# Last token group of a mixture of MLPs: second product by two nested Strassen levels

## The chip, the cores and the metric

The kernel runs on one core of a Trainium2 chip. The metric is the device time of one execution in microseconds, from the first instruction to the last. The kernel before takes 1227.81 us (median of three runs, 1226.56 to 1229.82). All arithmetic is in fp32.

The engines are named as in the profile: PE is the matrix engine, PEld its weight loads, DVE the vector engine, ACT the scalar engine, POOL the GpSimd engine, SP the engine that here only issues transfers. Each works through its own queue in order and waits on semaphores. PSUM is the memory that PE writes (8 banks of 128 x 512 fp32), SBUF the working memory, DRAM the device's main memory.

## The reference

Attention makes x, and four expert MLPs are applied to every token, mixed by normalised probabilities:

```python
def _moe_ref(x, domain_probs, w1, w2):          # x: 3072 x 512, w1: 4 x 512 x 1024, w2: 4 x 1024 x 512
    p = domain_probs / (domain_probs.sum(-1, keepdims=True) + 1e-09)
    out = np.zeros((N, D), dtype=np.float32)
    for e in range(E):
        h = np.maximum(x @ w1[e], 0.0)
        out += p[:, e:e + 1] * (h @ w2[e])
    return out
```

x comes from a decayed linear attention (4 batches, 8 heads, 768 positions, 64 per head), computed in blocks. The change doesn't touch it.

## The kernel before

**Tiling.** The 3072 tokens are three groups (`g`) of 1024. A group and an expert (`e`) make a unit, of which there are twelve, in the order (0,0), (0,1), ... (2,3). A unit has two matrix products: the first gives the hidden values h, transposed (1024 features x 1024 tokens), the second gives the outputs (1024 tokens x 512).

**Strassen.** A product of two matrices cut in 2 x 2 blocks can be done with seven block products M1 to M7 instead of eight, if sums of blocks are made first and the results are added up afterwards. `A_OF` and `B_OF` say which block or sum is an operand of which product (S1 to S4 are sums of left blocks, T1 to T4 of right blocks). The *first product* (`first_product`, L537) uses this twice, one inside the other: 7 outer products M, each of 7 inner ones (`inner`, L548), and each inner product is two matmuls of 128 x 128 by 128 x 256. Its operands with all their sums are prepared ahead by Pool (`prepare_w1`, L170; `prepare_x`, L236), written to DRAM (`inner`, L138, whose stores go out on ACT's queue) and read back by `feed` (L480). PE writes the PSUM banks pg; the values are added into SBUF tiles m by DVE (L93, called from `inner`), or copied by ACT where a sum begins (L563), and ReLU is applied by ACT (L567, L509).

The *second product* (`second_product`, L592) uses one level: 7 products, each of four parts (L594) of four matmuls, with h or its sums hS as the left operand (from `operands`, L458, on DVE) and w2 or its sums as the right (`prepare_w2`, L202; read by `feed2`, L577, 512 KB per product). A part is 128 tokens x 256 outputs. DVE scales it by the gate of the token, which stands on the partitions here, and adds it into the accumulators acc (L620, L623). After the last expert the accumulators are stored from Pool's queue (L626).

**The order of the work** is written out by hand. The loop over units at L734 pairs the second product of one unit with the first product of the next. It goes through seven steps `i`, one M of each; a step has eight slots, in which pieces of the two products alternate on PE (`order`, L755). After each slot one piece of background work runs on DVE (`rest`, L343: sums for S blocks, and sums that the outer Strassen level needs), every second slot `pump` (L127) issues pending stores and one chore of the operand preparation, and one step of the attention of a later group is put in where there is one. The attention of group 2 lies beside the units (0,3) to (1,1). The unit (2,3) has no first product beside it: it stands alone at the end.

**Buffers.** `stage` has 7 buffers of 128 x 1024 for preparing operands, `w2` has 6 for right operands, `stream` has 2 of each kind for the operands of the first product, `o` has 8 of 128 x 512 for acc, `pool` has 47 of 128 x 512 for everything else. Second products use the PSUM banks q01, q02, q11, q12, first products g1 and g3, attention s0 and s1.

`tt` (L92, its instruction on L93) is the helper for all sums of two tensors, so in the profile one line, L93, stands for many places. The tiles tell them apart.

Of the kernel before, what the change touches and what calls it, by code (L numbers as in the profile page):

```python
# [10 lines left out]
ALU = mybir.AluOpType  # L11
AX = mybir.AxisListType
FP32 = mybir.dt.float32
# [7 lines left out]
def kernel(  # L21
# [95 lines left out]
    x_ops = dram.tile([NG, 7, P, 7, 256], FP32, name="x_ops")  # L117
    w2_sums = dram.tile([E, 4, P, 2, W], FP32, name="w2_sums")

    W1_AT = {n: i for i, n in enumerate(("M1", "M7", "M6", "M5", "M3", "M2", "M4"))}  # L120
# [45 lines left out]
    def inner_x(eng, g, m, blk):  # L166
        at = {"B11": (0, 0), "B12": (0, 1), "B21": (1, 0), "B22": (1, 1)}
        inner(eng, ("x", g, m), x_ops[g, MS.index(m)], blk, T_OPS, at)

    def prepare_w1(e):  # L170
        st = {}

        def block(name, i, j):
            t = stage.tile([P, 2, W], FP32, name="w1b", tag="st")
            src = moe_w1[e, j * 256:(j + 1) * 256, i * W:(i + 1) * W]
            nc.sync.dma_start(out=t[:], in_=src.rearrange("(c p) f -> p c f", p=P))
            st[name] = t

        def total(name, a, b, op):
            t = stage.tile([P, 2, W], FP32, name="w1o", tag="st")  # L180
            tt(nc.gpsimd, t[:], st[a][:], st[b][:], op)
            st[name] = t

        def ready(m):
            inner_w1(e, m, st[A_OF[m]])

        return [
            lambda: (block("A11", 0, 0), block("A21", 1, 0), block("A22", 1, 1)),
            lambda: ready("M1"),
            lambda: total("S1", "A21", "A22", ALU.add), lambda: ready("M5"),  # L190
            lambda: total("S3", "A11", "A21", ALU.subtract), lambda: ready("M7"),
            lambda: (total("S2", "S1", "A11", ALU.subtract), block("A12", 0, 1)), lambda: ready("M6"),
            lambda: ready("M2"),
            lambda: total("S4", "A12", "S2", ALU.subtract), lambda: ready("M3"),
            lambda: ready("M4"),
        ]

# [4 lines left out]
    def prepare_w2(e):  # L202
# [8 lines left out]
        def total(name, n, a, b, op):  # L211
# [14 lines left out]
            lambda: total("T4", 3, "B21", "T2", ALU.subtract),  # L226
        ]

    SUM_AT = {"T1": 0, "T2": 1, "T3": 2, "T4": 3}
# [94 lines left out]
    gate = consts.tile([P, NTOK // P, E], FP32, name="gate")  # L324

    def gates():
        total = consts.tile([P, NTOK // P], FP32, name="total")
# [12 lines left out]

    background = []

    def rest(n=1):  # L343
        for _ in range(min(n, len(background))):
            background.pop(0)()

# [128 lines left out]


    SEQ = ("M1", "M5", "M6", "M2", "M7", "M3", "M4")
    fed = {}

    def feed(g, e, m):  # L480
        if (g, e, m) in fed:
            return
        while ("x", g, m) not in made and background:
            rest()
        until(("x", g, m))
# [6 lines left out]

    INNER = ("M1", "M7", "M6", "M4", "M5", "M2", "M3")

# [7 lines left out]
    def finished(g, e, m, blocks, new):  # L502

        def later(to, a, b, order, relu=False):
            def step(at):
                o = to[at] if at in to else small("m" + at)
                tt(nc.vector, o[:], a[at][:], b[at][:], ALU.add)
                if relu:
                    nc.scalar.activation(out=o[:], in_=o[:], func=AF.Relu)  # L509
                to[at] = o  # L510
                blocks["left"] -= 1
# [3 lines left out]

        def keep(c, i, j):
            hid[g, e, i, j] = {"A11": c["11"], "A12": c["21"], "A22": c["22"], "A21": c["12"]}
            operands((g, e, i, j))
# [13 lines left out]
    def settle(m, blocks):  # L532

        while m in ("M7", "M4") and blocks["left"]:
            rest()

    def first_product(g, e, m, blocks, tags):  # L537
# [10 lines left out]
        def inner(i):  # L548
# [17 lines left out]
            if m in OUT and (at == "12" or not begins):  # L566
                nc.scalar.activation(out=new[at][:], in_=new[at][:], func=AF.Relu)  # L567

        return [lambda i=i: inner(i) for i in INNER] + [lambda: finished(g, e, m, blocks, new)]
# [22 lines left out]
    def second_product(g, e, m, banks):  # L592

        def part(sj, s):  # L594
# [7 lines left out]
            for uu in range(2):  # L602
                h = hid[g, e, uu, sj]
                while A_OF[m] not in h:
                    rest()
                for c in range(2):
# [17 lines left out]
            if e == E - 1 and m in ("M2", "M4", "M5", "M3"):  # L624
                queue = nc.sync if (g, m) == (NG - 1, "M3") else nc.gpsimd
                queue.dma_start(out=out[n * P:(n + 1) * P, j * DH:(j + 1) * DH], in_=o)  # L626

# [6 lines left out]

        return [lambda sj=sj, s=s: part(sj, s) for s in range(2) for sj in (1, 0)] + [done]


# [93 lines left out]
    fill = [(*u, m) for u in units[2:] for m in SEQ]  # L731
    fill2 = [(*u, m) for u in units for m in SEQ2]
    steps = attention(1)
    for at, (g, e) in enumerate(units):  # L734
        if (g, e) == (0, 1) or (g, e) == (0, 2):
            chores.extend(prepare_w2(e + 1) + prepare_w1((e + 2) % E))
        if (g, e) == (0, 3):
            chores.extend(prepare_w1(1))
        ahead = units[at + 1] if at + 1 < len(units) else None
        if ahead and ahead[1] == 0:  # L740
            assert not steps
            steps = attention(ahead[0] + 1) if ahead[0] + 1 < NG else []
        blocks, banks = {}, {}
        for i in range(7):
            for _ in range(2 if at + i == 0 else 1):
                if fill2:
                    feed2(*fill2.pop(0))
            b = second_product(g, e, SEQ2[i], banks)
            a = []
# [3 lines left out]
            elif ahead:  # L753
                a = first_product(*ahead, SEQ[i], blocks, ("g1", "g3"))
            order = [a[0:2], b[0:1], a[2:4], b[1:2], a[4:6], b[2:3], a[6:8], b[3:5]]  # L755
            for x, part in enumerate(order):
                for f in part:
                    if f:
                        f()
                rest()  # L760
                if x == 0 and at * 7 + i >= 6 and fill:
# [3 lines left out]
                if steps and (at > 0 or i > 1) and (x == 5 or (x == 2 and i in (1, 3, 5) and at > 0)):  # L765
                    steps.pop(0)()
                if x % 2 == 0:
                    pump()
    assert not (background or chores or stores)

# [27 lines left out]
```

## Time and profile before

| stretch (us) | PE busy | DVE busy | ACT busy | POOL busy | DMA share |
|---|---|---|---|---|---|
| 0 to 135: attention of group 0, first products | 127.73 | 85.66 | 38.02 | 43.32 | 0.62 |
| 335 to 440: group 0, operands being prepared | 103.60 | 70.42 | 19.98 | 65.79 | 0.89 |
| 545 to 650: group 1 | 105.00 | 64.24 | 20.97 | 3.53 | 0.52 |
| 960 to 1060: group 2 | 100.00 | 61.92 | 16.23 | 0.00 | 0.48 |
| 1165 to 1225: last unit and what leads into it | 56.61 | 20.67 | 2.52 | 6.48 | 0.23 |

Each row gives busy microseconds of the engines within the stretch and the mean busy share of the sixteen DMA engines. A busy PE need not be a PE at its peak, since matmuls are pipelined and their ends are modelled. In a row of the profile's groups the columns are: line, engine, operation, output tile <- input tiles, shapes, number of instructions, then busy time, mean duration in ns, and the idle time just before them with what ended it. Names stand without buffer numbers. An fp32 matmul is two records in the trace.

### The profile page before, as it was taken

What the parts mean: (1) busy time and instruction counts of PE and PEld (TensorE: products, weight loads), DVE (VectorE), ACT (ScalarE), POOL (GpSimd) and SP (SyncE); (2) the same over time, 40 slices, a digit from 0 to 9 for tenths busy, and PEclk for the clock granted to TensorE, in tenths of its full rate; (3) what the DMA queues carried; (4) which work ended last, traced back from release to release, by engine and by line L of the source; (5) the groups of instructions that cost most, each with busy time, mean ns of one, the idle gap of its engine ahead of it and who ended that gap; (6) DMA issues with size and microseconds to landing.
All of it is one profiled execution on the core that took longest, in us unless ns stands there. A gap on an engine that the chain in (4) does not pass through costs nothing.

```text
span 1225.0 us, 16958 instructions
## 1 busy us (share of the span) xinstructions
PE 1209.3 (99%) x6696; PEld 1053.7 (86%) x6696; DVE 743.4 (61%) x1231; ACT 219.6 (18%) x385; POOL 305.5 (25%) x294
## 2 busy tenths in 40 slices
PE   8999998999999999999999999999999999999998
PEld 6888887888888888888888888888888888888887
DVE  5586575477567746746655755755755755745742
ACT  3322121112212211311220220220220220120100
POOL 4520365662481865120002600000100000000001
PEclk9999999999999999999999999999999999999999
DMA  9753679998998899666544855455564454554422
GB/s 235 195 158 117 221 249 357 356 357 279 339 345 274 289 345 365 229 210 224 183 169 163 308 188 199 155 201 203 184 237 171 171 216 155 188 199 155 172 70 85
DMA packets 174047, 273.15 MB, mean 223 GB/s; under 512 B 88208, under 2 KB 121616, under 8 KB 173968
## 3 DMA queue, kind: packets, MB, share of 16 engines
q1 hardware_dynamic: 145152, 212.89, 51.1%
q10 hardware_dynamic: 26704, 53.41, 11.4%
q0 software_dynamic: 2112, 5.77, 1.2%
q8 instruction: 53, 0.87, 0.3%
q14 instruction: 26, 0.21, 0.1%
HBM read 212.39 MB, written 59.64 MB: 222 GB/s over the span
## 4 chain that ended last, share of the span: by engine, by line
PE 92%; DMA 4%; POOL 2%; DVE 1%; ACT 0%; issue 0%; SPq 0%; POOLq 0%; DVEq 0%
PE q L607 44%; PE pg L555 34%; PE pM L656 5%; PE sp L382 2%; PE op L410 2%; PE kp L359 1%; PE op L405 1%; DMA w2t<-in_moe_w_dram 1%; PE qp L359 1%; POOL ops L93 1%; DMA w_ops<-w1b 1%; DMA w1b<-in_moe_w_dram 1%; PE op L418 1%; POOL w2o L93 1%; DVE hS L93 1%; DMA w_ops<-ops 0%
## 5 line engine op out<-in xcount | busy, mean ns | idle before, releaser
L555 PE MATMUL pg<-xs_in,ws_in 128*128 128x256 f32 x1960 | 472.6, 381 | 4.6 <-ACT m L563 3.2
L555 PEld LDWEIGHTS pg<-xs_in,ws_in 128*128 128x128 f32 x1960 | 370.4, 190 | 57.2 <-ACT m L563 3.6
L607 PE MATMUL q<-w2t,hS 128*128 128x256 f32 x1536 | 361.2, 379 | 0.0
L93 DVE TENSOR_TENSOR m<-pg,m 128x512 f32<-128x512 f32 x410 | 280.5, 689 | 107.6 <-PE pg L555 94.8
L607 PEld LDWEIGHTS q<-w2t,hS 128*128 128x128 f32 x1536 | 291.2, 190 | 39.9
L623 DVE SCALAR_TENSOR_TENSOR acc<-q,gate,acc 128x256 f32<-128x256 f32 x288 | 139.1, 483 | 249.5 <-PE q L607 249.0
L607 PE MATMUL q<-w2t,m 128*128 128x256 f32 x1152 | 271.1, 380 | 0.0
L607 PEld LDWEIGHTS q<-w2t,m 128*128 128x128 f32 x1152 | 218.8, 190 | 30.0
L626 POOL DMA_DIRECT2D out_dram<-acc x44 | 24.1, 548 | 544.8 <-DVE acc L623 544.8
L567 ACT ACTIVATE m<-m 128x512 f32<-128x512 f32 x120 | 75.4, 630 | 354.3 <-DVE m L93 328.6
L563 ACT COPY m<-pg 128x512 f32<-128x512 f32 x80 | 46.6, 587 | 167.5 <-PE pg L555 157.3
L93 DVE TENSOR_TENSOR hS<-m,m 128x512 f32<-128x512 f32 x96 | 67.5, 708 | 13.9 <-ACT m L567 13.9
L93 DVE TENSOR_TENSOR m<-m,m 128x512 f32<-128x512 f32 x96 | 71.0, 745 | 0.0
L509 ACT ACTIVATE m<-m 128x512 f32<-128x512 f32 x48 | 30.2, 630 | 151.8 <-DVE m L93 138.4
L93 POOL TENSOR_TENSOR kn<-kn,s_decay 128x512 f32<-128x512 f32 x20 | 23.8, 1192 | 103.0 <-PE kp L359 100.8
L620 DVE TENSOR_SCALAR acc<-q,gate 128x256 f32<-128x256 f32 x48 | 23.2, 483 | 41.0 <-PE q L607 40.9
L656 PE MATMUL pM<-xt,w1o 128*128 128x256 f32 x192 | 44.0, 381 | 0.6 <-DVE m L93 0.4
L93 DVE TENSOR_TENSOR m<-pM,m 128x512 f32<-128x512 f32 x40 | 27.4, 689 | 24.6 <-PE pM L656 24.5
L656 PEld LDWEIGHTS pM<-xt,w1o 128*128 128x128 f32 x192 | 36.1, 190 | 6.3 <-DVE m L93 0.8
L423 ACT COPY xT<-op 128x256 f32<-128x256 f32 x48 | 17.1, 373 | 118.6 <-PE op L410 90.9
L93 POOL TENSOR_TENSOR w2o<-w2b 128x1024 f32<-128x1024 f32 x8 | 19.6, 2457 | 71.7 <-DMA w2b<-in_moe_w_dram 43.5
L93 DVE TENSOR_TENSOR hS<-hS,m 128x512 f32<-128x512 f32 x48 | 37.1, 774 | 0.3
(64 smaller groups left out, 743.9 us busy)
## 6 DMA issues: line engine op xcount, KB each, us to landing
xs_in<-x_ops SPq DMA_DIRECT2D x70, 896.0 KB, 4.6
ws_in<-w_ops SPq DMA_DIRECT2D x70, 896.0 KB, 6.5
w2t<-w_sums SPq DMA_DIRECT2D x96, 256.0 KB, 6.4
w2t<-in_moe_w_dram SPq DMA_DIRECT2D x72, 256.0 KB, 6.4
w_ops<-ops ACTq DMA_DIRECT2D x28, 512.0 KB, 6.7
x_ops<-ops ACTq DMA_DIRECT2D x21, 512.0 KB, 5.3
w2b<-in_moe_w_dram SPq DMA_DIRECT2D x32, 256.0 KB, 4.9
w_sums<-w2o ACTq DMA_DIRECT2D x16, 512.0 KB, 5.3
```

What stands on the lines that cost most here:

```text
L93: eng.tensor_tensor(out=o, in0=a, in1=b, op=op)
L359: nc.tensor.transpose(out=x[:, ac * C:(ac + 1) * C], in_=y[:, 2 * ac:2 * ac + 2].rearrange("p r d -> p (r d)"), identity=ident[:],)
L382: nc.tensor.matmul(out=sp[r][:, ac * C:(ac + 1) * C], lhsT=hc(kT)[half[r], ac], rhs=hc(qT)[half[r], ac], start=True, stop=True,)
L410: nc.tensor.matmul(out=op[r][half[x], a * C:(a + 1) * C], lhsT=vn[:, 4 * r + 2 * a + x], rhs=hc(st[r])[:, 2 * a + x], start=(first and a = ...
L509: nc.scalar.activation(out=o[:], in_=o[:], func=AF.Relu)
L555: nc.tensor.matmul(out=p[:, j * 256:(j + 1) * 256], lhsT=ws[:, W1_AT[i], j * P:(j + 1) * P], rhs=xs[:, X_AT[i]], start=(fresh and j == 0), ...
L563: nc.scalar.copy(out=new[at][:], in_=p[:])
L567: nc.scalar.activation(out=new[at][:], in_=new[at][:], func=AF.Relu)
L607: nc.tensor.matmul(out=p[:, s * DH:(s + 1) * DH], lhsT=h[A_OF[m]][:, c * 256 + s * P:c * 256 + (s + 1) * P], rhs=fed2[g, e, m][uu][:, c], ...
L623: nc.vector.scalar_tensor_tensor(out=o, in0=x, scalar=w, in1=o, op0=ALU.mult, op1=ALU.add)
L626: queue.dma_start(out=out[n * P:(n + 1) * P, j * DH:(j + 1) * DH], in_=o)
L656: nc.tensor.matmul(out=p[:, s * 256:(s + 1) * 256], lhsT=a[c][:, f:f + P], rhs=b[:, c, j * 256:(j + 1) * 256], start=(s == 0 and c == 0), ...
```

## The change

In group 2 alone (`LAST`) the second product is done by two nested levels as well: 7 x 7 inner products of two matmuls instead of 7 x 16 matmuls. For this it is turned round: the left operand of PE (the weights that are loaded) is now w2 with its sums, the right one the hidden values of 256 tokens. The output then has the 512 output features on the partitions and the tokens along the columns. Three things follow:

- The gate of a token can no longer be applied by a scalar per partition. The gates are written to DRAM as rows (`gate_rows`), read back to all partitions (`gate_bc`), and multiplied into h by Pool after the ReLU (`gated`), so that the products of all four experts are simply added up.
- The sums of h for the outer level are made by DVE (`outer_sums`), those for the inner level by Pool (`inner_sums`), four per outer product, one outer product ahead.
- The outputs are added up over experts in seven tiles `sums`, one per M (they take the seven `stage` buffers). After the last expert these are added to each other (`join`), turned back by PE transposes, copied by ACT and stored (`give`).

The nested operands of w2 are prepared during the units of group 1 (`prepare_w2_ops`, on Pool, stores on ACT's queue, six per outer product) and read back by `feed3`. In groups 1 and 2 `pump` runs every third slot instead of every second, and the outputs of groups 0 and 1 are stored from ACT's queue instead of Pool's.

```diff
+    def inner_w2(e, m, blk):
...
+        for name, x, y, op in S_OPS:
+            b[name] = s[:, SLOT[name]]
+            tt(nc.gpsimd, b[name], b[x], b[y], op)
+        to = w2_ops[e, MS.index(m)]
+        stores.append(lambda: (
+            nc.scalar.dma_start(out=to[:, 0], in_=b["A11"]),
+            nc.scalar.dma_start(out=to[:, 1:3], in_=s[:, 0:2]),
+            nc.scalar.dma_start(out=to[:, 3], in_=b["A22"]),
+            nc.scalar.dma_start(out=to[:, 4], in_=b["S1"]),
+            nc.scalar.dma_start(out=to[:, 5], in_=b["A12"]),
+            nc.scalar.dma_start(out=to[:, 6], in_=b["S4"]),
+            made.add(("w2", e, m)),
+        ))
...
+    def gated(e, i, j, at, t):
+        def step():
...
+            tt(nc.gpsimd, x, x, by, ALU.mult)
+            outer[e][f"B{i + 1}{j + 1}"][at] = t
+        aside.append(after(2, step))
...
+    def outer_sums(e, *names):
...
+            tt(nc.vector, o[:], a[at][:], b[at][:], ALU.subtract)
...
+        background.extend(after(6, lambda n=n, at=at: total(n, at)) for n in names for at in BLOCKS)
...
+    def inner_sums(e, m, alone=True):
...
+            b[name] = opool.tile([P, W], FP32, name="acc")
+            tt(eng, b[name][:], b[x][:], b[y][:], ALU.subtract)
...
+        aside[0:0] = [functools.partial(parts[n], nc.gpsimd) for n in both]
...
-                queue = nc.sync if (g, m) == (NG - 1, "M3") else nc.gpsimd
-                queue.dma_start(out=out[n * P:(n + 1) * P, j * DH:(j + 1) * DH], in_=o)
+                stores.append(lambda: nc.scalar.dma_start(out=out[n * P:(n + 1) * P, j * DH:(j + 1) * DH], in_=o))
...
+    JOIN = {
+        "M1": (("M2", "M1"), ("M6", "M1")), "M5": (("M3", "M5"),),
+        "M6": (("M7", "M6"), ("M3", "M6"), ("M4", "M7"), ("M5", "M7")),
+    }
...
+    def give(m, t, tags):
...
+                nc.tensor.transpose(
+                    out=p[:, s * DH + dd * P:s * DH + (dd + 1) * P], in_=sums[m][:, 2 * dd + t, s * P:(s + 1) * P],
+                    identity=ident[:],
+                )
+        nc.scalar.copy(out=o[:], in_=p[:])
...
+    def nested_product(e, m, tags):
...
+            for c in range(2):
+                nc.tensor.matmul(
+                    out=p[:, 0:256], lhsT=fed3[e, m, x // 2][:, x % 2, c * P:(c + 1) * P],
+                    rhs=b[B_OF[i]][:, c * 256:(c + 1) * 256], start=(fresh and c == 0), stop=True,
+                    skip_group_check=True,
+                )
+            at, begins = READ[i]
+            o = sums[m][:, BLOCKS.index(at)]
+            if begins and e == 0:
+                nc.scalar.copy(out=o, in_=p[:, 0:256])
+            else:
+                tt(nc.vector, o, p[:, 0:256], o, ALU.add)
...
+            if nested:
+                order = [a[0:2], b[0:2], a[2:4], b[2:4], a[4:6], b[4:6], a[6:8], b[6:8]]
+            else:
+                order = [a[0:2], b[0:1], a[2:4], b[1:2], a[4:6], b[2:3], a[6:8], b[3:5]]
...
-                rest()
+                now[0] += 1
+                if joins:
+                    joined()
+                elif ahead or x % 2 == 0:
+                    rest()
+                if nested or nests:
+                    take(aside)
...
-                if x % 2 == 0:
+                if x % (2 if g == 0 else 3) == 0:
                     pump()
```

## The prediction

> **What bounds the kernel now.** I read the busy shares first, then who waited for whom on PE, then the chain that ended last, then the timeline of the last stretch, which is the one that the change rewrites.
>
> ```profile
> PE 1209.3 (99%) x6696; PEld 1053.7 (86%) x6696; DVE 743.4 (61%) x1231; ACT 219.6 (18%) x385; POOL 305.5 (25%) x294
> ...
> L607 PE MATMUL q<-w2t,hS 128*128 128x256 f32 x1536 | 361.2, 379 | 0.0
> ...
> L607 PE MATMUL q<-w2t,m 128*128 128x256 f32 x1152 | 271.1, 380 | 0.0
> ```
>
> PE is busy for 1209 of 1225 us, and the second product's matmuls (L607) never sat idle for anything. The list of PE's waits adds up to 12.0 us over the whole span, 4.5 of it the first load; the two largest in the main loop are:
>
> ```profile
> PE pg L555 <- ACT m L563: 3.2, 1, 3.2
> PE pg L555 <- DVE m L93: 1.4, 1, 1.4
> ```
>
> So PE's own instruction stream is the time, and a matmul taken out of it is worth its step. The step isn't the mean duration of 379 ns, since matmuls overlap. It stands in the timeline of the last unit, which has no first product beside it:
>
> ```profile
> 1173.10 13.98 PE L607 MATMUL q<-w2t,m 128*128 128x256 f32 x64
> ...
> 1186.91 13.98 PE L607 MATMUL q<-w2t,hS 128*128 128x256 f32 x64
> ```
>
> 64 records start 13.81 us before the next 64: 0.216 us each. One fp32 matmul of 256 columns is two records, 0.432 us.
>
> **What the skill says.** "Trainium Kernel Development and Optimization", Performance Expectations: matmul busy time is a bad metric because matmuls are pipelined. Agreed here: 379 ns of duration against 216 ns of step. "SBUF — State Buffer", Who interferes with whom: a VectorE instruction with two SBUF inputs contends with a GpSimd instruction that reads SBUF, one with at most one SBUF input doesn't. The trace agrees:
>
> ```profile
> 350.80 2.35 POOL L93 TENSOR_TENSOR w1o<-w1o,w1b 128x1024 f32<-128x1024 f32 x1
> ...
> 351.21 2.49 DVE L93 TENSOR_TENSOR qs<-qT,q_decay 128x512 f32<-128x512 f32 x1
> ```
>
> An SBUF-SBUF sum of 512 columns takes 0.68 us alone, and here 2.49, ending just after Pool's sum. "GPSIMD Engine Reference", 3.1 Elementwise: 4497 ns for a two-input add of 2048 elements; Pool's 1024-column sums here take 2.35 to 2.58 us, which is the same rate. "TensorE: Matmul & The Clock Gate", Part 4: a transpose goes to PSUM, so a copy must follow, and costs about 275 ns in context. The trace differs on the cost: qp's four transposes start at 574.88 and kp's four at 575.32, so one costs 0.11 us in a stream; I use 0.11.
>
> **The change, part by part.**
>
> *Matmuls removed.* A unit of group 2 had 7 products x 16 matmuls = 112 (224 records) for its second product; nested, it has 49 x 2 = 98 (196 records). Saved: 28 records x 4 units x 0.216 = 24.2 us, all on PE.
>
> *Transposes added.* 8 calls of the turning-back function x 4 = 32 transposes x 0.11 = 3.5 us, on PE in the last unit.
>
> *Tail.* Before, the last matmuls end at about 1222.4 and the span at 1225.0: 2.6 us for one 0.48 us scaling and one store (median 1.7 us to landing). After, the last sum (0.42, the 256-column PSUM sum kv<-kv,op) is followed by four transposes (0.44, counted above), a 512-column copy on ACT (0.59) and a store of twice the bytes (I take 2.3). With about 0.2 for each of three hand-overs that is 4.5 us: 1.9 more.
>
> *Pool.* Group 2's Pool was idle (0.0 us busy from 960 to 1060). It gets, per unit, 16 multiplications by the gates and 7 x 4 inner sums, all 512 columns: 44 x 1.06 to 1.19 us (kn<-kn,s_decay, in the window 335 to 440 and over the run) = 47 to 52 us of a unit of (196 + 196) x 0.216 = 84.7 us. In a product of 12.1 us it gets at most 8 (one of each slot): 9.5 us. So it keeps up, and the sums of the next product are made one product ahead. In the last unit only 4 are left per product: 4.8 of 6.05 us. No stall is taken for Pool as such.
>
> *VectorE.* Evictions of 128x256 grow from 28 to 49 per unit. Sums in a row cost less than their duration, since they overlap a little: from starts in the timeline, 0.62 us for 512 columns from PSUM, 0.60 for 512 from SBUF, 0.40 for today's scaling. For the 256-column sum I take 0.34 (0.42 less the same overlap). An overlapped unit then has 41 x 0.62 + 49 x 0.34 + 24 x 0.60 = 56.5 us of work in 84.7 us. But the 24 SBUF sums now stand beside a Pool that is 60% busy. The window 335 to 440, where Pool was 63% busy, shows what that does:
>
> ```profile
> L93 DVE TENSOR_TENSOR hS<-m,m 128x512 f32<-128x512 f32 x8 | 6.4, 802 | 0.7 <-ACT m L567 0.7
> L93 DVE TENSOR_TENSOR m<-m,m 128x512 f32<-128x512 f32 x8 | 5.9, 734 | 0.0
> ...
> L93 DVE TENSOR_TENSOR hS<-hS,m 128x512 f32<-128x512 f32 x4 | 4.9, 1233 | 0.0
> ...
> L93 DVE TENSOR_TENSOR hS<-m,hS 128x512 f32<-128x512 f32 x4 | 4.5, 1118 | 0.0
> ```
>
> The mean of these 24 is 0.90, 0.22 above the free value. That adds 5 us: VectorE is at 62 of 84.7, and PE in that window still had only 1.4 us of waits. The sums come in bursts, though (16 after M3 and M4), and a pair of inner products of each kind (3.45 us of PE) with two of them costs 2 x 0.62 + 2 x 0.34 + 2 x 0.60 to 1.05 = 3.1 to 4.0 us. Bounds: 0 to 3 us per unit; I take 2.5 us over the three units.
>
> *The last unit.* Here no first product hides anything, and VectorE holds PE directly: each inner product adds on a bank that the one before last must have been read from. Per product PE needs 28 x 0.216 = 6.05 us, VectorE 7 x 0.34 = 2.4 plus its SBUF sums. In the changed kernel's instruction order those are 26 in this unit, unevenly: about 5 in M1, 7 in M3, 4 in M5, 2 in M7, 1 in M6, 8 in M2 (the joins of the result blocks), none in M4. At 0.60 the excess over 6.05 is 0.6 in M3 and 1.2 in M2, 1.8 us; at 1.05 (each one meets a Pool sum) it is 1.6, 3.7, 0.6 and 4.7, 10.6 us. At 0.82 (0.22 more, as measured) it is 0.5, 2.1 and 2.9: 5.5 us. Taken: 5.5.
>
> *Group 1: the operands of w2.* Per expert Pool gets 4 sums of 1024 columns and 28 of 256: 4 x 2.4 + 28 x 0.8 = 32 us per unit, where it was busy 2 to 27 of 105 us. ACT gets 42 stores, in bursts of six: each holds the queue for 0.33 to 0.44 us, so 2 us and more, and behind it stand the copies and ReLUs (L563, L567, L509). DMA gets 2 MB read and 6.4 MB written per unit of about 105 us, 80 GB/s on top of about 200; PE was never held at 329 GB/s and a DMA share of 0.95 (235 to 335). The window 335 to 440 has about as many stores on ACT and cost PE 1.4 us. I take 0; high end of the fourth case below.
>
> *Edits at nothing.* The reads of the nested operands (7 x 128 KB per product instead of 512 KB) are asked for at least 10 inner products ahead, 8.6 us in the last unit, against 2.5 to 3.6 us to landing there now. Out stores of groups 0 and 1 move from Pool's queue to ACT's, off PE's path. Background work every third slot instead of every second: some 60 steps for the 84 slots of group 1. Gate rows: one small load per unit, asked for a product ahead.
>
> Sum: 1227.8 - 24.2 + 3.5 + 1.9 + 2.5 + 5.5 = **1217.0 us**.
>
> **The rivals.**
> *All hidden.* Pool sums rarely meet VectorE's, and PE stays the bound to the end: without the last two terms, 1209.0 us. For it speaks that PE stood at 100% in the worst stretches before; against it, eight joins in a product of 6 us don't fit.
> *VectorE takes it back.* Each SBUF sum meets a Pool sum: 10.6 in the last unit and 3 x 3 in the others: 1209.0 + 19.6 = 1228.6, no change. For it: a sum can be blocked for a whole Pool instruction (2.49 us above). Against it: at 63% Pool the mean loss was 0.22, not 0.45.
> *The stores hold ACT, slower.* If a quarter of the 28 bursts in group 1 blocks an eviction for 3 us, as ACT's waits behind w_ops of 6 to 12 us show is possible, that is 21 us: 1238. Against it: in group 0, with the same mechanism, PE lost 3.2 us to ACT in all. A Pool that falls behind the gates, with VectorE waiting on it and PE on VectorE, would end at the same place.
>
> **How the numbers follow.** Forecast 0.60, all hidden 0.19, taken back 0.10, slower 0.11. Of the third case 0.04 lies under 1224.1 (0.3% down), the rest within 0.3%, and so does 0.01 of the fourth. Faster: 0.60 + 0.19 + 0.04 = 0.83; same 0.06 + 0.01 = 0.07; slower 0.10. The range reaches down to the second case less 2 us, 1207, and up to the third, 1228.6.
>
> **What would show it.** Right: PE records 112 fewer for the second product plus 32 transposes, and the units (2,0) to (2,2) about 6 us shorter each. The last unit keeps its 50 us or so, with PE waiting on VectorE's sums in M3 and M2. Wrong: PE waits on Pool's acc tiles or the gated blocks; waits on ACT in group 1; VectorE's 256-column sum at 0.5 us instead of 0.34, which alone would add 49 x 0.16 = 8 us per unit of VectorE time and make it the bound of the last one.

## The result, and the profile after

The changed kernel takes 1242.2 us (median of 4 runs, 1241.8 to 1242.8) against 1227.2 us before (1226.6 to 1229.8): ratio 1.0118, 95% interval 1.0101 to 1.0136. It is slower by 1.2%, where 1217.0 us was forecast.

The busy shares, the second product's rows and Pool's largest new row on the page of the changed kernel:

```profile
PE 1198.4 (97%) x6616; PEld 1032.4 (83%) x6616; DVE 815.3 (66%) x1301; ACT 232.4 (19%) x421; POOL 647.4 (52%) x554
...
L829 PE MATMUL pq<-acc,w2t 128*128 128x256 f32 x448 | 111.7, 384 | 6.6 <-issue 3.1
...
L94 POOL TENSOR_TENSOR m<-m,gate_bc 128x512 f32<-128x512 f32 x64 | 85.6, 1354 | 60.7 <-ACT m L687 34.4
```

PE has 80 records fewer, as counted (112 matmul records less 32 transposes), and is 11 us less busy, yet the span is 15.7 us longer (1240.7 against 1225.0). So PE now waits. The list of its waits on the changed kernel (waiting tile <- who released it: us in all, times, longest):

```profile
PE pg L675 <- ACT m L683: 12.1, 4, 10.2
PE pq L829 <- DVE sums L94: 5.5, 5, 1.3
PE pg L675 <- DVE m L94: 4.5, 5, 1.8
...
PE pq L829 <- issue: 3.1, 4, 1.2
PE pq L829 <- POOL acc L94: 2.2, 1, 2.2
PE pq L829 <- ACT m L687: 2.0, 1, 2.0
```

One wait of 10.2 us stands out, and a scatter of short ones in the nested product. To see where the time lies I cut both traces into units. ACT begins a sum by copying the first values of a first product, eight such copies per unit, so the first of each eight marks where a unit starts. The time from mark to mark, named by the second product in it (us):

| kernel | (1,0) | (1,1) | (1,2) | (1,3) | (2,0) | (2,1) | (2,2) and (2,3) |
|---|---|---|---|---|---|---|---|
| before | 105.3 | 96.9 | 90.7 | 90.6 | 90.7 | 90.6 | 141.5 |
| after | 117.4 | 99.2 | 91.1 | 91.8 | 87.9 | 87.8 | 149.8 |

The three stretches of group 0 ahead of these differ by 0.1 to 1.9 us. The overlapped nested units are faster, by 2.8 us each. The last stretch is 8.3 us slower, and the unit that stands alone is what makes it so: from the end of the last first product to the end of the span 53.5 us before, 64.7 after. And (1,0), in which nothing nested runs on PE, is 12.1 us slower. So there are two separate places to explain.

*The unit (1,0).* ACT's timeline (start, duration, what it did, idle time before it) and the entry in the chain that ended last, changed kernel:

```profile
516.96 0.54 ACTq L956 DMA_DIRECT2D gate_rows<-gate  x1
...
530.75 0.59 ACT L683 COPY m<-pg 128x512 f32<-128x512 f32 x1 [0.28 <-PE pg L675]
544.63 0.38 ACTq L246 DMA_DIRECT2D w_ops<-w2b  x1
...
547.75 0.59 ACT L683 COPY m<-pg 128x512 f32<-128x512 f32 x1 [16.41 <-DMA w_ops<-ops]
```

```profile
516.96 27.66 DMA gate_rows<-gate
```

The store of the gates is 16 KB and takes 27.66 us. ACT's next store goes out at 544.63, and 516.96 + 27.66 is 544.62. Six stores follow in a burst, and behind them on the same queue comes the copy that PE needs, after 16.41 us in which ACT did nothing else. It isn't Pool that the burst waited for: Pool's last sum for w2's operands before it ended at 535.2. PE, same stretch:

```profile
532.28 1.89 PE L675 MATMUL pg<-xs_in,ws_in 128*128 128x256 f32 x8
...
536.19 1.99 PE L729 MATMUL q<-w2t,m 128*128 128x256 f32 x8
548.39 3.64 PE L675 MATMUL pg<-xs_in,ws_in 128*128 128x256 f32 x8 [10.21 <-ACT m L683]
```

The wait costs more than its own length. The granted clock was 0.50 from 541.5 to 551.8, into the first 3.4 us after the wait, and the eight records there took 3.64 us where eight took 1.89 before. 10.21 and 1.75 are 12.0 of the 12.1 us.

*The unit that stands alone.* Four neighbouring lines of the timeline of VectorE, Pool and PE in it:

```profile
1188.51 2.98 DVE L94 TENSOR_TENSOR sums<-sums 128x512 f32<-128x512 f32 x2
...
1189.35 3.27 POOL L94 TENSOR_TENSOR acc<-hT,acc 128x512 f32<-128x512 f32 x2
...
1191.93 1.97 PE L829 MATMUL pq<-acc,w2t 128*128 128x256 f32 x8 [2.21 <-POOL acc L94]
...
1195.22 1.13 PE L829 MATMUL pq<-acc,w2t 128*128 128x256 f32 x4 [1.33 <-DVE sums L94]
```

Two sums of SBUF blocks on VectorE last 2.98 us, 1.49 each instead of 0.68, and the two of Pool beside them 1.64 each. PE waits first for Pool's, then for VectorE's. The groups of the stretch 1000 to 1090, in overlapped units of the changed kernel, show the same at length:

```profile
L94 DVE TENSOR_TENSOR hT<-m,m 128x512 f32<-128x512 f32 x10 | 12.0, 1210 | 0.0
L94 POOL TENSOR_TENSOR acc<-hT,acc 128x512 f32<-128x512 f32 x8 | 10.8, 1353 | 2.0 <-PE pq L829 1.5
```

My theory was then: the store of the gates costs 8 to 12 us, and Pool's sums and VectorE's SBUF sums slow each other, which costs the nested units the rest; edits that take either away should give its share back. The rivals: that PE waits for Pool's results as such (Pool is too slow, whoever else runs); that VectorE has too much to do even undisturbed; that preparing w2's operands is what costs group 1.

### The profile page after: what moved, and what is told of

It reads as the page before. It is cut to its first block, busy times and chain, and to the rows that moved or that the text cites. A ratio compares the mean times of both kernels' runs of the same rounds, so it can differ in the third digit from the quotient of the medians.

```text
span 1240.7 us, 17846 instructions
## 1 busy us (share of the span) xinstructions
PE 1198.4 (97%) x6616; PEld 1032.4 (83%) x6616; DVE 815.3 (66%) x1301; ACT 232.4 (19%) x421; POOL 647.4 (52%) x554
## 4 chain that ended last, share of the span: by engine, by line
PE 78%; DMA 8%; DVE 7%; POOL 4%; issue 1%; ACT 1%; ACTq 0%; SPq 0%; POOLq 0%; DVEq 0%
PE pg L675 29%; PE q L729 24%; PE pq L829 12%; PE pM L867 5%; DVE hT L94 3%; POOL ops L94 2%; DMA gate_rows<-gate 2%; PE sp L442 2%; DVE m L94 2%; PE op L470 2%; DMA w2t<-w_sums 1%; DVE sums L94 1%; DMA w2b<-in_moe_w_dram 1%; PE qp L419 1%; PE kp L419 1%
## 5 line engine op out<-in xcount | busy, mean ns | idle before, releaser
L675 PE MATMUL pg<-xs_in,ws_in 128*128 128x256 f32 x1960 | 475.3, 382 | 16.8 <-ACT m L683 12.1
L729 PE MATMUL q<-w2t,hS 128*128 128x256 f32 x1024 | 242.5, 380 | 0.0
L729 PEld LDWEIGHTS q<-w2t,hS 128*128 128x128 f32 x1024 | 193.9, 190 | 26.7
L745 DVE SCALAR_TENSOR_TENSOR acc<-q,gate,acc 128x256 f32<-128x256 f32 x192 | 92.5, 482 | 147.7 <-PE q L729 147.0
L729 PE MATMUL q<-w2t,m 128*128 128x256 f32 x768 | 181.7, 379 | 0.0
L729 PEld LDWEIGHTS q<-w2t,m 128*128 128x128 f32 x768 | 145.6, 190 | 20.0
L829 PE MATMUL pq<-acc,w2t 128*128 128x256 f32 x448 | 111.7, 384 | 6.6 <-issue 3.1
L94 POOL TENSOR_TENSOR m<-m,gate_bc 128x512 f32<-128x512 f32 x64 | 85.6, 1354 | 60.7 <-ACT m L687 34.4
L829 PEld LDWEIGHTS pq<-acc,w2t 128*128 128x128 f32 x448 | 84.9, 192 | 21.2 <-POOL acc L94 4.7
L94 DVE TENSOR_TENSOR sums<-pq,sums 128x256 f32<-128x256 f32 x168 | 69.1, 419 | 40.7 <-PE pq L829 37.0
L829 PE MATMUL pq<-hT,w2t 128*128 128x256 f32 x192 | 48.5, 379 | 0.0
```

The source lines that it names most:

```text
L94: eng.tensor_tensor(out=o, in0=a, in1=b, op=op)
L675: nc.tensor.matmul(out=p[:, j * 256:(j + 1) * 256], lhsT=ws[:, W1_AT[i], j * P:(j + 1) * P], rhs=xs[:, X_AT[i]], start=(fresh and j == 0), ...
L729: nc.tensor.matmul(out=p[:, s * DH:(s + 1) * DH], lhsT=h[A_OF[m]][:, c * 256 + s * P:c * 256 + (s + 1) * P], rhs=fed2[g, e, m][uu][:, c], ...
L745: nc.vector.scalar_tensor_tensor(out=o, in0=x, scalar=w, in1=o, op0=ALU.mult, op1=ALU.add)
L829: nc.tensor.matmul(out=p[:, 0:256], lhsT=fed3[e, m, x // 2][:, x % 2, c * P:(c + 1) * P], rhs=b[B_OF[i]][:, c * 256:(c + 1) * 256], start= ...
```

## The experiments

All times are medians with the ratio to the kernel before and its 95% interval; the kernel before was run again beside each set, with medians from 1226.9 to 1228.1 us. Unit times are read as in the table above, from one traced run each, which need not be the median one.

### Group 1: the store of the gates, and the preparation

**The gates turned first.** One PE transpose makes 32 rows of 128 gates, and the store is 32 pieces of 512 B ahead of the units.

```diff
+    nc.tensor.transpose(out=gp[0:32, 0:P], in_=gate[:, LAST * CPG:].rearrange("p n e -> p (n e)"), identity=ident[:])
+    nc.scalar.copy(out=gs[0:32, 0:P], in_=gp[0:32, 0:P])
+    nc.scalar.dma_start(out=gate_rows[:].rearrange("n e p -> (n e) p"), in_=gs[0:32, 0:P])
...
-                chores.append(lambda: nc.scalar.dma_start(
-                    out=gate_rows[:].rearrange("n e p -> p (n e)"), in_=gate[:, LAST * CPG:].rearrange("p n e -> p (n e)"),
-                ))
```

> The gates of the last group are turned on PE (one transpose) and stored as 32 rows of 512 bytes, early, instead of 4096 pieces of 4 bytes at the start of group 1. Theory (the slow store, 27.7 us to landing, holds ACT's later stores, and ACT then holds PE): the unit with (1,0) comes back from 117.4 to about 106 us and the whole to about 1231 us. Rival (the bursts of six stores of w2 operands hold ACT, whatever the gates do): that unit stays above 113 us and the whole above 1238 us.

Measured: 1234.17 us, ratio 1.0055 (1.0036 to 1.0074), 8.0 us less than the changed kernel. Unit (1,0) falls from 117.4 to 105.6. The later stretches stay within 0.9 us; (0,1) takes 109.8 for 107.0, but it lies anywhere from 107.0 to 110.4 over all the traces. The store's row among the DMA issues (KB, us to landing) in the changed kernel and here:

```profile
gate_rows<-gate ACTq DMA_DIRECT2D x1, 16.0 KB, 27.7
```

```profile
gate_rows<-gs ACTq DMA_DIRECT2D x1, 16.0 KB, 1.4
```

The same 16 KB land in 1.4 us. So more than half of the loss against before (15.0 us) is this one store. The edit changes its form and its place together, so it doesn't tell what an early store in 4-byte pieces would cost. What is left, 7 us above before, has other causes.

**The slow store alone**, put into the kernel before:

```diff
+        if (g, e) == (1, 0):
+            chores.append(lambda: nc.scalar.dma_start(
+                out=gate_rows[:].rearrange("n e p -> p (n e)"), in_=gate[:, 2 * CPG:].rearrange("p n e -> p (n e)"),
+            ))
```

> The kernel before with one thing added, the gates' store of 4096 pieces of 4 bytes at the start of group 1; nothing reads it. Theory (the store is slow, and the cost comes when ACT's next stores have to wait for it): group 1 has few stores on ACT here, so the cost is under 4 us. Rival (the slow store holds ACT's queue or the transfers by itself): 8 us or more.

Measured: 1228.11 us, ratio 1.0006 (0.9994 to 1.0018): next to nothing, though the store took 18.8 us here. Its length isn't the cost. In this kernel ACT's next DMA is due at 542.6, after the store has landed at 541.6, and the copies in between (525.5 to 541.9) run on time. In the changed kernel the stores of w2's operands come due in the meantime. What costs is what stands behind the store in ACT's order. This run's DMA queue line (packets, MB) against that of before also tells what the store is made of:

```profile
q10 hardware_dynamic: 30816, 53.43, 12.1%
```

```profile
q10 hardware_dynamic: 26704, 53.41, 11.4%
```

4112 packets more: 8 columns x 4 experts x 128 partitions are 4096 elements, one packet of 4 bytes for each. What the other 16 are, the run doesn't tell.

**The preparation alone**: the kernel before with w2's nested operands prepared in group 1 (sums, stores, the pump at every third slot), and nothing that uses them.

```diff
-    LAST = NG - 1
+    LAST = NG
...
-        if g == LAST - 1:
+        if g == 1:
```

> The kernel before, with the preparation of the nested w2 operands in group 1 added (Pool sums, bursts of six stores, every third slot), which nothing reads, and without the gates' store. Theory (the preparation alone costs little; what is lost in group 1 is the gates' store): 1227 to 1231 us. Rival (bursts hold ACT, and ACT holds PE): 1235 us or more.

Measured: 1230.15 us (20 runs), ratio 1.0025 (1.0015 to 1.0036): 3 us, not nothing. The traced run (1228.84) is one of the quicker ones, and its span is 1.8 us longer than that of before; all of that is in unit (1,1), 98.7 for 96.9. (1,0) stays at 105.4. Where the rest of the 3 us lies isn't shown. So the store alone costs about nothing and the preparation alone 3 us, but the store on top of the preparation 8.0.

### Group 2: Pool, VectorE, or PE waiting for Pool

**No gate products.** Pool's 16 multiplications per unit are left out, so the experts are added up without their gates; the slow gate store is in.

```diff
-            tt(nc.gpsimd, x, x, by, ALU.mult)
```

> The 64 multiplications of h by the gates on Pool are left out (so the output is not weighted by the gates in the last group); all else is as in the change. Theory (SBUF sums of VectorE and Pool take turns, so that 24 on VectorE and 44 on Pool fill the unit): the units (2,0) to (2,2) shrink from 88 to about 85 us each, VectorE's SBUF sums fall from 1.1 to under 0.9 us, the whole to about 1233 us. Rival (the overlapped units lose their gain to the finer evictions, 49 instead of 28): no change there, above 1239 us.

Measured: 1237.53 us (1233.5 to 1246.9), ratio 1.0088 (1.0061 to 1.0114). Overlapped units 86.6 and 86.0 for 87.9 and 87.8; last stretch 143.4 for 149.8.

**No inner sums in the last unit** (plain blocks of h in their place; slow gate store in):

```diff
+            if e == E - 1:
+                b[name] = b[{"T1": "B11", "T2": "B12", "T3": "B21", "T4": "B22"}[name]]
+                return
             b[name] = opool.tile([P, W], FP32, name="acc")
```

> In the last expert of the last group Pool makes no inner sums; plain blocks stand in for them (so the output is wrong there in value, with the same matmuls). Theory (the last unit is bound by SBUF sums of Pool and VectorE in turns): it falls from 64.8 to about 54 us, the whole to about 1231 us. Rival (the last unit is bound by VectorE's own evictions and joins, or by the hand-over from PE to VectorE and back at every inner product): it stays at 61 us or more, the whole above 1238 us.

Measured: 1242.48 us, ratio 1.0111 (1.0093 to 1.0130): no gain in the median, though in its trace the last stretch falls to 142.4 as much as it does without the gate products; (1,0) is at 119.7 there, 2.3 above the changed kernel's. With that store in, a gain of this size isn't settled by the whole time, so the further kernels have the gates turned.

**No joins.** The 14 sums of result blocks in the last unit are left out, on top of the turned gates.

```diff
-                for x in JOIN.get(m, ()):
-                    join(*x)
+                pass
```

> With the gate rows turned (1234.2 us), the 14 joins of the result blocks are left out (so the output lacks these terms). Theory (about half of the last unit's loss is VectorE's bursts of joins among its evictions): the last unit 5 to 7 us shorter, the whole about 1228 us. Rival (Pool's inner sums are all of it): less than 2 us.

Measured: 1228.39 us, ratio 1.0003 (0.9989 to 1.0016); last stretch 142.6 for 150.6 with the turned gates alone. 14 sums at 0.68 are 9.5 us of VectorE, at the measured 0.975 13.7; leaving them out saves 8.0 us of the last stretch and 5.8 of the whole. Leaving out the gate products, the inner sums or the joins saves 6.4, 7.4 and 8.0 us of the last stretch, together 21.8, more than its whole excess over before (8.3). So the effects don't add. That fits turns taken between VectorE and Pool, of which any one can be shortened; these three runs alone don't prove it.

**No work for Pool**, neither gates nor any inner sum, on top of the turned gates (plain blocks, no gates, as above):

```diff
-            tt(nc.gpsimd, x, x, by, ALU.mult)
...
-            b[name] = opool.tile([P, W], FP32, name="acc")
-            tt(eng, b[name][:], b[x][:], b[y][:], ALU.subtract)
+            b[name] = b[{"T1": "B11", "T2": "B12", "T3": "B21", "T4": "B22"}[name]]
```

> Gate rows turned, and Pool makes neither the gates' products nor the inner sums in the last group (plain blocks stand in, so the output is wrong in value there; the matmuls are the same). Theory (what the units (2,0) to (2,2) lose beside their matmuls is Pool's hold on VectorE's SBUF sums): these units at 84.7 to 85.5 us. Rival (VectorE's 49 evictions in short steps hold PE by themselves): above 86.5 us.

Measured: 1219.57 us, ratio 0.9932 (0.9913 to 0.9951). Overlapped units 85.8, last stretch 139.6. Pool costs 14.6 us (1234.2 less 1219.6). One overlapped stretch of 85 us of the changed kernel and one of this (busy us and instructions of PE, PEld, DVE, ACT and POOL, granted clock, DMA share, GB/s):

```profile
1003.00:1088.00 85.00, 83.79 (x385) 72.25 (x384) 66.79 (x111) 14.11 (x23) 57.02 (x43) 1.00 0.62 229
```

```profile
985.00:1070.00 85.00, 85.00 (x390) 73.18 (x389) 61.20 (x112) 14.46 (x26) 0.00 (x0) 1.00 0.63 230
```

Without Pool, PE never idles, and VectorE does one instruction more in 5.6 us less.

**Pool's work kept, its results unread.** This separates slowing from waiting. Pool does the same 44 operations per unit but writes into a buffer that nobody reads (`dump()` hands out parts of xT, which is free by then); everything else is as without Pool's work, plain blocks and no gates.

```diff
-            tt(nc.gpsimd, x, x, by, ALU.mult)
+            tt(nc.gpsimd, dump().rearrange("p (c t) -> p c t", c=2), x, by, ALU.mult)
...
-            b[name] = opool.tile([P, W], FP32, name="acc")
-            tt(eng, b[name][:], b[x][:], b[y][:], ALU.subtract)
+            b[name] = b[{"T1": "B11", "T2": "B12", "T3": "B21", "T4": "B22"}[name]]
+            tt(eng, dump(), b[x][:], b[y][:], ALU.subtract)
```

> The gate rows turned as in the first experiment, and Pool does the same 44 operations of 512 columns per unit from the same inputs, but writes them into a buffer that nobody reads: the second product takes plain blocks of h in place of the inner sums, and the gates are left out of the values. So Pool's reads of SBUF stand beside VectorE's sums as before, but no engine waits for a result of Pool. Theory (what Pool costs is VectorE's sums and Pool's slowing each other): units (2,0) and (2,1) stay at 87.5 to 88 us, VectorE's sums of two SBUF blocks stay at 1.0 to 1.2 us, the whole is 1229 us or more. Rival (the cost is PE and VectorE waiting for Pool's results): units at 85.8 us and the whole near 1220 us, as with no Pool work at all (1219.6). In the last unit both may count: there the theory expects most of the 9 us to stay.

Measured: 1238.28 us (1235.9 to 1240.7), ratio 1.0084 (1.0057 to 1.0112); units 87.9 and 88.6, last stretch 151.9. All of Pool's cost is back though no engine uses a result of Pool's, and in the trace no wait of PE, VectorE or ACT from 850 us on is put down to Pool. It is even 4.1 us more than with the turned gates alone, with intervals that overlap; why is open. VectorE's SBUF sums, over 985 to 1070, in this kernel and without Pool's work:

```profile
L94 DVE TENSOR_TENSOR hT<-m,hT 128x512 f32<-128x512 f32 x8 | 10.8, 1366 | 0.0
L94 DVE TENSOR_TENSOR hT<-m,m 128x512 f32<-128x512 f32 x8 | 9.7, 1232 | 0.0
```

```profile
L94 DVE TENSOR_TENSOR hT<-m,m 128x512 f32<-128x512 f32 x8 | 5.3, 682 | 0.0
L94 DVE TENSOR_TENSOR hT<-m,hT 128x512 f32<-128x512 f32 x8 | 5.3, 682 | 0.0
```

PE's waits from 985 to the end, here and in the changed kernel:

```profile
PE pq L835 <- DVE sums L94: 9.3, 8, 2.2
```

```profile
PE pq L829 <- DVE sums L94: 4.2, 4, 1.3
...
PE pq L829 <- POOL acc L94: 2.2, 1, 2.2
```

What was a wait for Pool becomes one for VectorE. The rival, that PE waits for Pool's results as such, isn't needed for the cost: Pool's work beside VectorE's sums brings it by itself.

### Can the contention be taken out?

**The gate on VectorE.** ReLU and gate in one VectorE instruction instead of ACT's ReLU and Pool's multiplication, on top of the turned gates.

```diff
-            tt(nc.gpsimd, x, x, by, ALU.mult)
+            nc.vector.scalar_tensor_tensor(out=x, in0=x, scalar=0.0, in1=by, op0=ALU.max, op1=ALU.mult)
```

> With the gate rows turned as in the first experiment (1234.2 us), ReLU and gate become one VectorE instruction (max with 0, times the gate), so that ACT's 16 ReLUs and Pool's 16 products per unit fall away and VectorE gets 16 x 0.6 us more. Theory (VectorE and Pool hold each other up through their SBUF sums, and the chain ACT, Pool, VectorE at the end of a unit delays the next one): units (2,0) and (2,1) from 87.9 to about 86.5 us, the last two together from 150.6 to about 145, the whole to about 1227 us. Rival (VectorE's own load is the bound of these units): no gain or a loss, 1234 us or more.

Measured: 1260.98 us, ratio 1.0270 (1.0244 to 1.0296), so the idea falls. In a stretch of 94 us of overlapped units, and among PE's waits:

```profile
1000.00:1094.00 94.00, 87.84 (x397) 73.72 (x396) 78.41 (x130) 5.06 (x9) 39.64 (x29) 1.00 0.58 211
```

```profile
PE pq L831 <- DVE sums L94: 14.5, 15, 2.1
```

Pool is 42% busy instead of 67%, but VectorE is 78.4 of 94 us busy, and PE waits for it 15 times. Against the turned gates alone (2,0), (2,1) and the last stretch lose 4.3, 6.1 and 3.5 us. Here contention is cheaper than a full VectorE. Another 9.5 us of this trace lie in (1,3) (102.2 for 92.7), where PE waited once for 5.6 us for a read of first-product operands (ws_in) and not for VectorE; why that read came late isn't known.

**One level for the last expert** (w2 still on the left), on top of the turned gates: 14 additions of 512 columns from PSUM on VectorE instead of 49 of 256, and no inner sums on Pool in the unit that stands alone, for 28 more matmul records. In this first form one block is turned back before its last sum is in.

```diff
-                b = nested_product(e, SEQ3[i], (("q01", "q02"), ("q11", "q12"))[i % 2])
+                b = (nested_product if ahead else single_product)(e, SEQ3[i], (("q01", "q02"), ("q11", "q12"))[i % 2])
```

> With the gate rows turned (1234.2 us), the last expert alone is done with one level, turned round as the change has it: 112 matmuls instead of 98 (6.0 us more of PE), no inner sums on Pool, 14 evictions of 512 columns instead of 49 of 256. Theory (in the last unit PE waits on VectorE and Pool, more than the second level saves): the last unit from about 65 to 57 us, the whole to about 1226 us. Rival (what holds the last unit is the joins and turning back, which stay): 1234 us or more.

Measured: 1228.91 us, ratio 1.0011 (0.9998 to 1.0024). Last stretch 144.7 for 150.6.

**Both, and alternating banks** between successive units (line against the kernel just above):

```diff
-                b = (nested_product if ahead else single_product)(e, SEQ3[i], (("q01", "q02"), ("q11", "q12"))[i % 2])
+                b = (nested_product if ahead else single_product)(e, SEQ3[i], (("q01", "q02"), ("q11", "q12"))[(e + i) % 2])
```

> Both together, and the PSUM banks alternate across the border of two units too (the first outer product of a unit no longer reuses the banks of the last one of the unit before). Theory: the gains add, about 1219 us, faster than the kernel before. Rival (they are the same waits, counted twice): 1225 us or more.

Measured: 1242.69 us, ratio 1.0115 (1.0094 to 1.0136). The gate on VectorE spoils this one too (units at 91.8 and 93.9, but (1,3) at 93.4, without the wait for ws_in).

**Alternating banks alone**, with the turned gates:

```diff
-                b = nested_product(e, SEQ3[i], (("q01", "q02"), ("q11", "q12"))[i % 2])
+                b = nested_product(e, SEQ3[i], (("q01", "q02"), ("q11", "q12"))[(e + i) % 2])
```

> Gate rows turned (1234.2 us) and only the banks alternating across the border of two units. Theory (at each border PE waits about 2 us because the same two banks are used twice in a row): about 3 us less per border seen in the last two units and 1 in the others, 1229 us. Rival: no change.

Measured: 1236.64 us, ratio 1.0067 (1.0041 to 1.0094), last stretch 151.4: nothing gained. The banks were not the wait.

**One level for the last expert and alternating banks**, with every block finished before it is turned back (the additions go by token half, so that the first half is done first; line against the first form above):

```diff
-                o = sums[m][:, 2 * i:2 * i + 2].rearrange("p k t -> p (k t)")
+                o = sums[m][:].rearrange("p (i k) t -> p i k t", k=2)[:, :, t]
```

> Gate rows turned, last expert with one level, each block finished before it is turned back, and the PSUM banks alternating across the border of two units. Theory: as in e6 the last unit takes about 54 us, and the first outer product of a unit no longer waits on the evictions of the last: 1225 us, a little under the kernel before. Rival (the wait at the border is VectorE's queue and not the bank): no gain over e6, 1228 us.

Measured: 1225.97 us (18 runs), ratio 0.9987 (0.9976 to 0.9998). It is quicker than the changed kernel by 16 us and than the one before by 1 us, which the interval only just allows. The part after the last first product:

```profile
1167.00:1224.00 57.00, 52.58 (x259) 45.93 (x257) 28.62 (x44) 5.12 (x9) 2.99 (x2) 1.00 0.26 83
```

against the nested one of the changed kernel:

```profile
1176.00:1240.00 64.00, 50.63 (x233) 40.69 (x231) 47.04 (x79) 5.12 (x9) 39.39 (x27) 0.97 0.39 119
```

28 more PE matmul records by the program, and shorter: 57.6 us for 64.7. VectorE is busy 29 us instead of 47. The groups of the two stretches, the nested one first, tell how much of that is fewer additions, and how much that its sums run less disturbed, the joins at 685 ns instead of 975:

```profile
L94 DVE TENSOR_TENSOR sums<-pq,sums 128x256 f32<-128x256 f32 x50 | 20.4, 418 | 13.0 <-PE pq L829 12.8
L94 DVE TENSOR_TENSOR sums<-sums 128x512 f32<-128x512 f32 x14 | 13.1, 975 | 0.1
```

```profile
L94 DVE TENSOR_TENSOR sums<-pq,sums 128x512 f32<-128x512 f32 x14 | 9.7, 690 | 24.0 <-PE pq L834 24.0
L94 DVE TENSOR_TENSOR sums<-sums 128x512 f32<-128x512 f32 x14 | 8.8, 685 | 0.1
```

The additions fall from 20.4 us to 9.7, so some 11 of the 18 us are fewer additions. The other 7 or so are sums of two SBUF blocks that last less long: the joins (13.1 to 8.8 us) and the outer sums (15.9 to 10.7; durations overlap a little).

**The pump's pace.** The version just above with the pump back at every second slot in all groups:

```diff
-                if x % (2 if g == 0 else 3) == 0:
+                if x % 2 == 0:
```

> The version with one level for the last expert and alternating banks (1225.97 us), with pending stores and preparation issued every second slot in all groups, as before the change, instead of every third in groups 1 and 2. Theory (the cost of preparing w2's operands in group 1 is their stores and sums as such, not the slower pace): unit (1,1) stays within 1 us of 100.8 and the whole within 0.2% of 1226. Rival (the slower pace delays the preparation of later operands and what waits for them): unit (1,1) back to about 97 us and the whole near 1222 us.

Measured: 1232.77 us (22 runs), ratio 1.0039 (1.0029 to 1.0050). Neither expectation holds: unit (1,1) is back at 97.0, from 100.8, as the rival said, but (1,2) goes from 91.2 to 96.7 and the whole is 6.8 us slower. The traced run (1228.63) is among the quickest of the 22 and only 2.5 us longer in its span than the trace it is compared with, so most of the 6.8 us isn't placed. ACT in (1,2):

```profile
739.28 0.38 ACTq L254 DMA_DIRECT2D w_ops<-w2o  x1
740.30 0.33 ACTq L255 DMA_DIRECT2D w_ops<-ops  x1
746.75 0.38 ACTq L256 DMA_DIRECT2D w_ops<-w2o  x1
...
748.80 0.59 ACT L691 COPY m<-pg 128x512 f32<-128x512 f32 x1 [9.53 <-DMA w_ops<-w2o]
```

A burst of stores stops half way for 6.4 us, and a copy stands behind it; PE waits 3.6 us. In these traces the stores' pace moves their cost from one unit to another, and by the whole times the slower pace is the better one.

## Why the prediction was wrong, point by point

**Gate rows, "one small load per unit", at nothing: this step failed, by 8.0 us.** I costed the load of the gates and overlooked the store. It was in the diff, `out=gate_rows[:].rearrange("n e p -> p (n e)")`, and its innermost step in DRAM is 128 elements. The Trainium skill, "DMA: Bandwidth & Descriptors", Rules for kernel authors, says that a strided last dimension becomes one descriptor per element and is to be rearranged; the 4112 packets and the 1.4 us of the turned version agree. Nor did I ask what stands behind that store on ACT's queue: six stores and a copy. It cost 8.0 us of the whole time, 11.8 in the trace of (1,0). The rival "the stores hold ACT" names this wait, with 21 us from the 28 bursts of w2's stores; those alone cost 3. So that rival's time of 1238, nearest to the result, was near it by luck: the cost came from a single store that no case had.

**Pool and VectorE, 2.5 + 5.5 us: right in kind, too small, and the largest miss.** 8.0 us were forecast for all that VectorE holds PE up. Pool's work alone costs 14.6, and some 7 more remain without it (see the sum below). "SBUF — State Buffer", Who interferes with whom, which I had cited, holds: sums with two SBUF inputs last 1.5 times as long in the mean, while those with one input from PSUM don't move (m<-pg,m 688 ns beside Pool, 690 without). What failed is the size that I took from the window 335 to 440: 0.22 us for each sum. In the overlapped units it was 0.37: 682 ns without Pool, and with the turned gates, over 985 to 1070, the mean of these 24, 1053 ns:

```profile
L94 DVE TENSOR_TENSOR hT<-m,m 128x512 f32<-128x512 f32 x8 | 9.7, 1226 | 0.0
L94 DVE TENSOR_TENSOR hT<-m,hT 128x512 f32<-128x512 f32 x8 | 8.8, 1118 | 0.0
L94 DVE TENSOR_TENSOR m<-m,m 128x512 f32<-128x512 f32 x8 | 6.5, 814 | 0.0
```

The joins had 975 against 685, so 0.29. The means hide that the loss comes in lumps: of the 14 joins of the changed kernel eight took 0.67 to 0.68 us, the other six 1.02 to 1.75. And the loss goes both ways, as that page says of issue order, which decides who blocks: Pool's 512-column operations, taken at 1.06 to 1.19 us, have means of 1.35 to 1.62 by kind and stretch. Part of this isn't contention but the price: I took it from kn<-kn,s_decay, and the inner sums' own median is 1.27. Pool was busy 57 of 85 us. The step "VectorE is at 62 of 84.7" was 67, still with room. So what failed in the overlapped units was the 2.5 us allowed for PE's meeting VectorE's sums; that it is their coming in bursts was argued, not tried. Those units gained 2.8 us each where 5.2 were forecast, 7 us less in all three, and the last unit lost 11.2 where 4.9 were forecast. (The list of that unit's sums by product adds up to 27, not 26; the trace has 28.)

**Group 1, "I take 0": wrong, by 3 us.** The preparation alone costs 1.0025 (1.0015 to 1.0036). Its DMA and Pool's share are as in group 0, but here the bursts of six stores stand ahead of copies that PE needs. The line "PE was never held at a DMA share of 0.95" was read in group 0, where a burst is three stores (L146 to L148 before), not six. That the six are the reason is argued from this and was not tried.

**Right:** PE's step and the 28 records per unit (85.8 us for a unit without Pool, where 84.7 was worked out); the transposes (four in 0.44 us again); the 256-column sum, 0.42 us; the reads of nested operands, for which PE never waited. The skill's 275 ns for a transpose, from which I said that the trace differs, is a duration; the 32 transposes at the end last 273 ns in the median and only start closer together, so page and trace don't disagree.

**Right in part by luck:** the tail. It took 5.0 us from the end of the last L829 matmul (1235.68) to the end of the span, where I used 4.5 and a transpose group of 0.44. But the pieces that I named for the 4.5 (0.42, 0.59, 2.3 and three times 0.2) add up to 3.9, so a slip of 0.6 made the figure fit.

**The sum.** Without Pool's work and with the gates turned: 1219.6, where 1209.0 was worked out for all hidden. 3 of the 10.6 between them are group 1's preparation; some 7 us remain, 5 of them in the last stretch (139.6, where 141.5 - 2 x 6.05 + 3.5 + 1.9 = 134.8 is what the forecast has without any hold), and the rest in units that are 1 us longer than their matmuls. In that last stretch PE waits 2.2 us for VectorE's sums, which run undisturbed there; the rest of the 5 isn't split up. Add 14.6 for Pool's work: 1234.2. Add 8.0 for the store: 1242.2. Not settled: 0.3 to 2.7 us more than before in (1,3) in most traces, with or without Pool's work, and why ACT's next store waits for the slow one to land: the two times agree to 0.01 us, but no run here tells whether it is the order of one queue or a semaphore.

## What to carry to other kernels

Cost every DMA that a diff adds by its innermost contiguous piece, not by its bytes, and then by what stands behind it on the engine that issues it: 16 KB in 4-byte pieces cost 8 us where six stores and a copy stood behind them on the queue, and nothing that could be measured (1.0006, interval across 1) where nothing was due before they had landed. Work given to an idle Pool isn't free if VectorE has two-input SBUF sums beside it: price both sides from a stretch with the same sizes, and try it by letting Pool do the work into a buffer that nobody reads. Where a unit has no other work beside it, more matmuls with fewer sums can be the shorter form.

## What the runs showed of the hardware that was not expected

- A store of 4096 pieces of 4 bytes took 27.7 us in one kernel and 18.8 in another; as 32 pieces of 512 B, at 95.6 us of the span and so amid other traffic, 1.4 us.
- A VectorE sum of two 128 x 512 SBUF blocks goes from 0.68 to means of 0.8 to 1.4 us, by kind, beside a Pool that is two thirds busy, and Pool's from 1.27 (at 1209.25 in the changed kernel, alone for a moment) to 1.35 to 1.62. These are lumps: eight of the 14 joins of the changed kernel ran free, six took 1.02 to 1.75 us.
- A burst of stores on ACT's queue stopped half way in one trace, 6.4 us between two of its issues.
- PE's long wait in (1,0) was paid for twice: the granted clock of the changed kernel fell to 0.50 at 541.5, 3.3 us into the wait of 10.2, and stayed there until 3.4 us after it. The 0.97 of the unit that stands alone is such a piece too, 3.4 us at 0.50 from 1179.8 among 1.00; in both, matmuls started about twice as far apart (0.425 us for 0.216). What sets it off, these runs don't tell.
